# A fused attention and mixture kernel on one core: the inner weight w_in is loaded, multiplied and used by quarters of its columns

## The chip, the cores and the metric

The kernel runs on one core of one Trainium2 chip, as one program. The metric is the device time of that program in microseconds (us), the median of three runs. TensorE is called PE in the profile, its weight loads PEld, VectorE DVE, ScalarE ACT, GpSimd POOL; SP is the engine whose queue issues the loads and stores.

## The reference

Three stages follow each other; every size is fixed.

```python
# attention: q, k, v of 4 batches, 8 heads, 1152 positions, 64 wide
q_pool = q.reshape(B, H, S // 2, 2, D).mean(axis=3)
attn = softmax(q_pool @ k.T / sqrt(D)); x = (attn @ v)        # -> x: 2304 tokens x 512
# soft mixture: phi 512 x 32, w1 8 x 512 x 1024, w2 8 x 1024 x 512
logits = x @ phi
slot_input = softmax(logits, axis=0).T @ x                    # 32 slots x 512
slot_out = relu(slot_input[e] @ w1[e]) @ w2[e]                # 4 slots for each of 8 e
x = softmax(logits, axis=1) @ slot_out                        # 2304 x 512
# feed-forward: w_in 512 x 2048, w_out 2048 x 512
h = x @ w_in
g = where(h >= 1, h, where(h <= -1, 0, (h + 1) ** 2 / 4))
return g @ w_out                                              # 2304 x 512
```

## The kernel before, in words

The attention (up to about 505 us of the span) and the softmax statistics are not touched by the change. What follows them is one pass with this order.

**Weights.** `w_load` issues the loads of w1, w2 and w_in on SP's queue in the order of `wlist`, 1 MB each, into 2048-column slots that come free one after the other (`w_used`). w_in and w_out come in as float64; during the attention they are turned into float32 and stored to two scratch tensors in device memory, `wi_dr` and `wo_dr` (`cv_step`), from which they are loaded again at the end.

**Slots.** `h1` multiplies the slot inputs with w1, `ht_mm` transposes the result on PE, `s2o(e, x)` multiplies with w2. `soT` is the transposed slot output, 128 x 4 x 32.

**M.** Since x = c @ slot_out has rank 32, x @ w_in is computed as c @ M with M = slot_out @ w_in, a 32 x 2048 matrix. The products of L916 make it as 4 groups of 32 rows by 512 columns, from all of `soT` and all four chunks of w_in; ACT copies it rounded (`Mhi`), DVE takes the rest (`Mlo`), and `Mrep(j)` spreads one group of 512 columns over the 128 partitions by a product with a selection matrix `Sel`, and copies it to `Mst`. `cT` is the transposed c, made by `c_xpose(n)` for thirds of the tokens.

**Feed-forward.** The tokens run in 9 blocks n of 256 (`TB`), the 2048 hidden columns in quarters qd of four chunks f of 128. `h_unit(n, qd)` makes h for a quarter (4 products on PE, two ReLU on ACT, two clamps on DVE), `g_unit` squares on ACT and adds on DVE, `g_split` rounds g on ACT (`ghi`) and subtracts on POOL (`glo`). The first eight chunks of block 0 go in six smaller pieces, `first_unit(i)`. Its call i does the front part of piece i and the end (add, round, subtract) of piece i - 1, so that call 6 only ends piece 5. `w_split(f0, f1)` rounds rows of w_out on ACT into `whi` and subtracts on DVE or POOL into `wlo`, in place. An output tile of 128 tokens is the sum over 16 chunks of three products, ghi with whi, ghi with wlo and glo with whi: `o_first(0, pos, f)` for the first four chunks of block 0, `o_part(n, tt, qd)` for all else, 12 products each.

**What sets the order.** Each engine works through its instructions in the order in which this code issues them and waits in order. `ahead(k)` runs the units of the list `units` up to number k in front of the output products; `FIRST`, `AHEAD` and `RUN` are its numbers. `warm_o` issues products that nobody reads.

## Time and profile before

| what | us |
|---|---|
| median of 3 runs (786.8 to 788.6) | 787.86 |
| the profiled execution, its own time | 788.76 |
| its span in the profile | 787.0 |
| PE busy in the span | 758.0 |
| DVE busy | 565.5 |
| ACT busy | 451.6 |
| POOL busy | 146.1 |

Busy times are sums over the whole span; the stretch that the change touches, some 45 us between 546 and 592 us, has to be read by itself.

### The profile page before, as it was taken

To read this page: it belongs to the slowest core of one execution; us is meant where nothing else is said; L and a number is where in the kernel's file an instruction comes from. 1 tells how busy PE (TensorE), PEld (TensorE's weight loads), DVE (VectorE), ACT (ScalarE), POOL (GpSimd) and SP (SyncE) were. 2 spreads that over 40 slices of the span, in tenths; PEclk is the share of its full clock that TensorE was granted. 3 is DMA by queue.
4 is the path that set the end of the run, shared out by engine and by line. 5 is a ranking of instruction groups with operands and counts; after the bars stand their busy time and mean duration, and the time that the engine had idled before them with its cause. 6 is when DMAs were issued, how large, how long until landed. Compare 5 with 4: busy or idle time off the path is not lost.

```text
span 787.0 us, 19058 instructions
## 1 busy us (share of the span) xinstructions
PE 758.0 (96%) x7896; PEld 557.9 (71%) x7896; DVE 565.5 (72%) x869; ACT 451.6 (57%) x855; POOL 146.1 (19%) x114
## 2 busy tenths in 40 slices
PE   7799999999999999999999999999789999999998
PEld 6677776766776766766766776633578888888887
DVE  6989889778889788889788883151697777666620
ACT  4347566666667566667575566401587777555620
POOL 7000000000000000000000000002574444443330
PEclk9999999999999999999999999999989999999999
DMA  8976767867789877899878826799600000000000
GB/s 215 203 185 167 190 185 189 225 187 204 196 217 246 214 179 164 232 184 241 230 175 202 220 89 235 271 333 395 241 0 27 28 28 17 11 27 27 27 28 27
DMA packets 138263, 127.11 MB, mean 162 GB/s; under 512 B 80576, under 2 KB 100288, under 8 KB 137408
## 3 DMA queue, kind: packets, MB, share of 16 engines
q1 hardware_dynamic: 138176, 125.89, 59.2%
q8 instruction: 62, 1.02, 0.5%
q14 instruction: 25, 0.20, 0.1%
HBM read 87.10 MB, written 13.11 MB: 127 GB/s over the span
## 4 chain that ended last, share of the span: by engine, by line
PE 84%; ACT 5%; DMA 4%; DVE 4%; issue 2%; SPq 1%; ACTq 0%; DVEq 0%
PE st L368 17%; PE acc L397 16%; PE mx L302 9%; PE po L1024 8%; PE po L1023 8%; PE po L1025 8%; PE acc L390 5%; ACT e L373 3%; DMA wi<-wi_dr 2%; PE h L960 2%; PE h L767 2%; PE tx L434 2%; ACT xnr L450 1%; PE tb L461 1%; DVE mp L314 1%
## 5 line engine op out<-in xcount | busy, mean ns | idle before, releaser
L373 ACT ACTIVATE e<-st 128x576 f32<-128x576 f32 x288 | 187.6, 652 | 147.6 <-PE st L368 142.9
L314 DVE TENSOR_REDUCE mp<-mx 128x1 f32<-128x576 f32 x282 | 211.0, 750 | 53.6 <-PE mx L302 50.4
L397 PE MATMUL acc<-e,vf 128*64 128x288 f32 x1152 | 198.0, 410 | 0.3 <-ACT e L373 0.3
L302 PE MATMUL mx<-K,q 128*64 128x288 f16 x1152 | 126.5, 294 | 11.5 <-ACT e L373 4.5
L368 PE MATMUL st<-q,K 128*64 128x288 f16 x1152 | 123.7, 287 | 4.1 <-DVE mp L314 2.5
L368 PE MATMUL st<-q,S 128*64 128x288 f16 x1152 | 123.7, 286 | 0.0
L302 PEld LDWEIGHTS <-q 128*64 128x64 f16 x1152 | 67.6, 110 | 69.4 <-issue 27.3
L1023 PE MATMUL po<-whi,ghi 128*128 128x512 f32 (+1 forms) x280 | 108.6, 388 | 0.0
L1024 PE MATMUL po<-wlo,ghi 128*128 128x512 f32 (+1 forms) x280 | 108.5, 388 | 0.0
L1025 PE MATMUL po<-whi,glo 128*128 128x512 f32 (+1 forms) x280 | 108.1, 386 | 0.0
L973 DVE TENSOR_TENSOR r<-cl,r 128x1024 f32<-128x1024 f32 x34 | 80.9, 2380 | 36.8 <-ACT cl L972 36.8
L979 POOL TENSOR_TENSOR glo<-r,ghi 128x1024 fp32r<-128x1024 f32 x34 | 82.1, 2414 | 95.4 <-ACT ghi L978 95.4
L270 POOL TENSOR_TENSOR qf<-qf 128x576 f32<-128x576 f32 x14 | 20.1, 1437 | 382.5 <-DMA qf<-in_q_dram 260.4
L397 PEld LDWEIGHTS acc<-e,vf 128*64 128x64 f32 x1152 | 80.3, 137 | 8.5 <-ACT e L373 2.4
L368 PEld LDWEIGHTS <-K 128*64 128x64 f16 x1152 | 70.2, 109 | 21.9 <-issue 12.7
L368 PEld LDWEIGHTS <-S 128*64 128x64 f16 x1152 | 71.4, 110 | 2.7
L380 DVE TENSOR_TENSOR es<-es,e 128x576 f32<-128x576 f32 x96 | 71.4, 745 | 2.6 <-ACT e L373 2.5
L963 ACT ACTIVATE r<-h,cols 128x512 f32<-128x512 f32 x68 | 42.9, 684 | 31.9 <-PE h L960 31.7
L1025 PEld LDWEIGHTS po<-whi,glo 128*128 128x128 f32 x280 | 53.2, 190 | 10.7
L1023 PEld LDWEIGHTS po<-whi,ghi 128*128 128x128 f32 x280 | 53.5, 191 | 9.9
L1024 PEld LDWEIGHTS po<-wlo,ghi 128*128 128x128 f32 x280 | 53.3, 190 | 9.5
L964 DVE TENSOR_SCALAR cl<-h 128x512 f32<-128x512 f32 x68 | 43.8, 685 | 15.6 <-ACT r L963 14.1
(192 smaller groups left out, 845.2 us busy)
## 6 DMA issues: line engine op xcount, KB each, us to landing
w<-in_moe_w_dram SPq DMA_DIRECT2D x31, 1024.0 KB, 7.6
vf<-in_v_dram SPq DMA_DIRECT2D x16, 576.0 KB, 5.0
kf<-in_k_dram SPq DMA_DIRECT2D x30, 288.0 KB, 3.8
f<-in_moe_w_out_dram SPq DMA_DIRECT2D x16, 512.0 KB, 5.2
f<-in_moe_w_in_dram SPq DMA_DIRECT2D x16, 512.0 KB, 5.8
qf<-in_q_dram SPq DMA_DIRECT2D x30, 256.0 KB, 4.6
S<-K SPq DMA_DIRECT2D x16, 288.0 KB, 6.2
out_dram<-ob SPq DMA_DIRECT2D x17, 256.0 KB, 2.0
```

The costliest lines, as they stand in the source:

```text
L302: nc.tensor.matmul(ps[p0:p1, i, 0:HQ], lhsT=q1[P][:, t, p0:p1], rhs=kk[:, j * HQ:(j + 1) * HQ], start=True, stop=True)
L314: nc.vector.tensor_reduce(out=mp[P][:, t, a:a + 1], in_=ps[:, :, 0:HQ], op=ALU.max, axis=AX.XY)
L368: nc.tensor.matmul(ps[c0:c0 + 64, i, 0:HQ], lhsT=kk[:, ci, c0:c0 + 64], rhs=f[:, sl[i]], start=first, stop=not first)
L373: nc.scalar.activation(out=e, in_=ps[:, :, 0:HQ], func=AF.Exp, scale=ESC)
L380: nc.vector.tensor_tensor(out=Es[P, n, h], in0=a, in1=b, op=ALU.add)
L397: nc.tensor.matmul(acc[P, i][h * 64:(h + 1) * 64, 0:HQ], lhsT=vt[P][:, h, c, :], rhs=E[P, c, h][:, i, :], start=(c == 0), stop=(c == NK - ...
L964: nc.vector.tensor_scalar(out=cl[:, a:b], in0=src, scalar1=-1.0, scalar2=1.0, op0=ALU.max, op1=ALU.min)
L973: nc.vector.tensor_tensor(out=r[:, sl], in0=cl[:, sl], in1=r[:, sl], op=ALU.add)
L979: nc.gpsimd.tensor_tensor(out=glo[n, qd][:, sl], in0=r[:, sl], in1=ghi[n, qd][:, sl].bitcast(F32), op=ALU.subtract)
L1023: nc.tensor.matmul(po, lhsT=ghi[n, qd][:, j, sl], rhs=whi[:, f, cs], start=(f == 0), stop=False)
L1024: nc.tensor.matmul(po, lhsT=ghi[n, qd][:, j, sl], rhs=wlo[:, f, cs], start=False, stop=False)
L1025: nc.tensor.matmul(po, lhsT=glo[n, qd][:, j, sl], rhs=whi[:, f, cs], start=False, stop=(f == 15))
```

## The change

w_in is stored in `wi_dr` by quarters of its 2048 columns, and each of its four loads now brings one quarter of the columns of all 512 rows. They go in turn with quarters of w_out: w_in 0, w_out 0, w_in 1, w_out 1, and so on; w_in 1 and 2 land for a while in rows of `whi` that are written only later, w_in 3 in a tile of its own. M is made by quarters: `M_piece(q)` makes 512 of its columns (as 4 groups of 128), copies and subtracts, and `Mrep(q)` spreads them, 8 products of 128 columns, with one copy by DVE. So the hidden columns of a quarter qd need M's quarter qd alone. Pieces 0 and 1 come before the output products, 2 and 3 between them; `quarter(q)` runs the units (0, 2) and (0, 3) with the w_out rows that belong to them. w2 is loaded with four consecutive rows to a partition (8 KB in one run), for which the transposes of `ht_mm` read columns 4 apart. Half of the copies of `c_xpose` go from ACT to DVE; one row of `warm_o` falls away.

```diff
--- before.py
+++ after.py
@@ -101,9 +101,9 @@
     LASTW = ("w1", 1, 0)
     wlist = [(kind, e, x) for kind in ("w1", "w2") for x in range(2) for e in range(E_) if (kind, e, x) != LASTW]
     wlist.insert(NSL, LASTW)
-    wlist += [("wi", dc, 0) for dc in range(4)]
+    wlist += [("wi", 0, 0)]
     wo_dr = dr_p.tile([128, 16, DM], F32, name="wo_dr")
-    wi_dr = dr_p.tile([4, 128, DFF], F32, name="wi_dr")
+    wi_dr = dr_p.tile([128, 4, 4, 512], F32, name="wi_dr")
     wt = {}
     nloaded, gone = 0, set()
 
@@ -121,17 +121,11 @@
             src = w1[e, :, x * 512:(x + 1) * 512].rearrange("(c p) f -> p c f", p=128)
             vw = t.rearrange("p (c f) -> p c f", c=4)
         elif kind == "w2":
-            src = w2[e, x * 512:(x + 1) * 512, :].rearrange("(c p) d -> p c d", p=128)
+            src = w2[e, x * 512:(x + 1) * 512, :].rearrange("(p c) d -> p c d", p=128)
             vw = t.rearrange("p (c d) -> p c d", c=4)
         else:
-            src, vw = wi_dr[e], t
-        if i < len(wlist) - 1:
-            nc.sync.dma_start(out=vw, in_=src)
-        else:
-
-            for hf in range(2):
-                a, b = [y.rearrange("p (j n) -> p j n", j=4)[:, :, hf * 256:hf * 256 + 256] for y in (vw, src)]
-                nc.sync.dma_start(out=a, in_=b)
+            src, vw = wi_dr[:, e], t.rearrange("p (c n) -> p c n", c=4)
+        nc.sync.dma_start(out=vw, in_=src)
         wt[kind, e, x] = vw
 
     def w_used(*keys):
@@ -205,7 +199,7 @@
                 nc.sync.dma_start(out=wo_dr[:, n, :], in_=dst)
             else:
                 dc, qr = divmod(n - 16, 4)
-                nc.sync.dma_start(out=wi_dr[dc][:, qr * 512:(qr + 1) * 512], in_=dst)
+                nc.sync.dma_start(out=wi_dr[:, qr, dc, :], in_=dst)
             if n + 3 < 32:
                 cv_load(n + 3)
 
@@ -773,8 +767,9 @@
         def ht_mm(i):
             htp[i] = sc_tile("ht0")[:, 0, :] if i == 0 else hp_tile("ht1")
             for kc in range(4):
-                nc.tensor.transpose(out=htp[i][:, kc * 128:(kc + 1) * 128], in_=h1s[i][:, kc * 128:(kc + 1) * 128],
-                                    identity=ident)
+
+                nc.tensor.transpose(out=htp[i][:, kc * 128:(kc + 1) * 128],
+                                    in_=h1s[i].rearrange("p (n k) -> p k n", k=4)[:, kc, :], identity=ident)
 
         def ht_sum(i):
             nc.vector.tensor_reduce(out=HT[:, 4 * i:4 * i + 4], in_=htp[i].rearrange("p (k d s) -> p k s d", k=4, d=4),
@@ -806,7 +801,10 @@
                     nc.tensor.transpose(out=ps[:, t * TT:(t + 1) * TT],
                                         in_=CN[:, n * 8 + 4 * i + t].rearrange("p r s -> p (r s)"), identity=ident[0:TT, 0:TT])
                 c0 = n * 768 + i * 384
-                nc.scalar.activation(out=cT[:, c0:c0 + 384], in_=ps[:, 0:384], func=AF.Copy)
+                if i:
+                    nc.vector.tensor_copy(cT[:, c0:c0 + 384], ps[:, 0:384])
+                else:
+                    nc.scalar.activation(out=cT[:, c0:c0 + 384], in_=ps[:, 0:384], func=AF.Copy)
 
         def s2o(e, x):
 
@@ -885,11 +883,21 @@
                 for r in range(4):
                     src = ident[:, 32 * j:32 * j + 32] if r // 2 == hl else zcol.to_broadcast([128, 32])
                     nc.gpsimd.tensor_copy(Sel[:, hl, j, 32 * r:32 * r + 32], src)
+
+        def wi_load(q_, t):
+            nc.sync.dma_start(out=t, in_=wi_dr[:, q_].rearrange("p c n -> p (c n)"))
+            wt["wi", q_, 0] = t.rearrange("p (c n) -> p c n", c=4)
+
+        def wo_load(q_):
+            nc.sync.dma_start(out=wlo[:, 4 * q_:4 * q_ + 4, :].bitcast(F32), in_=wo_dr[:, 4 * q_:4 * q_ + 4, :])
+
+        for q_ in range(3):
+            if q_:
+
+                wi_load(q_, whi[:, 4 * q_ + 4:4 * q_ + 8, :].bitcast(F32).rearrange("p f d -> p (f d)"))
+            wo_load(q_)
         for e in range(E_):
             s2o(e, 1)
-        pieces = [(0, 2), (2, 4), (4, 8), (8, 12), (12, 16)]
-        for f0, f1 in pieces:
-            nc.sync.dma_start(out=wlo[:, f0:f1, :].bitcast(F32), in_=wo_dr[:, f0:f1, :])
 
 
         def w_split(f0, f1):
@@ -905,25 +913,29 @@
         nc.vector.tensor_copy(soT, over_slots(hp_tile("soT"), S2sb))
         acc_x.close()
         po_p = ctx.enter_context(tc.tile_pool(name="po", bufs=4, space=PS))
-        Mp = [po_tile(f"M{i}")[:, 0:DM // 2] for i in range(2)]
+        for n in (1, 2):
+            c_xpose(n)
         wps = po_tile("warm_o")
-        for dc in range(4):
-            if dc < 2:
-                c_xpose(1 + dc)
-            for i in range(2):
-                for j in range(4):
-                    c0 = j * 512 + i * 256
-                    nc.tensor.matmul(Mp[i][32 * j:32 * j + 32], lhsT=soT[:, dc, :],
-                                     rhs=wt["wi", dc, 0][:, c0:c0 + 256], start=(dc == 0), stop=(dc == 3))
         Mst = x_p.tile([128, NTT * DM], F32R, tag="xn", name="Mst")
         Mhi, Mlo = Mst[:, DFF:DFF + DM], Mst[:, DFF + DM:DFF + 2 * DM]
-        HF = [slice(0, DM // 2), slice(DM // 2, DM)]
-        for i, sl in enumerate(HF):
-            nc.scalar.activation(out=Mhi[:, sl], in_=Mp[i], func=AF.Copy)
-            nc.vector.tensor_tensor(out=Mlo[:, sl], in0=Mp[i], in1=Mhi[:, sl].bitcast(F32), op=ALU.subtract)
-
+
+
+        def M_piece(q_):
+            ps = hp_tile(f"M{q_}")[:, 0:128]
+            for dc in range(4):
+                for j in range(4):
+                    nc.tensor.matmul(ps[32 * j:32 * j + 32], lhsT=soT[:, dc, :],
+                                     rhs=wt["wi", q_, 0][:, dc, j * 128:(j + 1) * 128], start=(dc == 0), stop=(dc == 3))
+            sl = slice(q_ * 128, (q_ + 1) * 128)
+            nc.scalar.activation(out=Mhi[:, sl], in_=ps, func=AF.Copy)
+            nc.vector.tensor_tensor(out=Mlo[:, sl], in0=ps, in1=Mhi[:, sl].bitcast(F32), op=ALU.subtract)
+
+        M_piece(0)
         w_split(0, 2)
         wx.close()
+        wi3_p = ctx.enter_context(tc.tile_pool(name="wi3", bufs=1))
+        wi_load(3, wi3_p.tile([128, 2048], F32, name="wi3"))
+        wo_load(3)
 
 
         g_p = ctx.enter_context(tc.tile_pool(name="g", bufs=6))
@@ -933,16 +945,13 @@
         NBK = NT // TB
         ghi, glo, hq = {}, {}, {}
 
-        def Mrep(j, parts):
-            for i, sl in enumerate(parts):
-                ps = hp_tile(f"Mr{j}_{i}")[:, 0:sl.stop - sl.start]
+        def Mrep(q_):
+            ps = hp_tile(f"Mr{q_}")
+            for j in range(4):
                 for hl, src in enumerate((Mhi, Mlo)):
-                    nc.tensor.matmul(ps, lhsT=Sel[:, hl, j, :], rhs=src[:, sl], start=(hl == 0), stop=(hl == 1))
-                dst = Mst[:, j * 512 + sl.start:j * 512 + sl.stop]
-                if (i + j) % 2 == 0:
-                    nc.vector.tensor_copy(dst, ps)
-                else:
-                    nc.scalar.activation(out=dst, in_=ps, func=AF.Copy)
+                    nc.tensor.matmul(ps[:, j * 128:(j + 1) * 128], lhsT=Sel[:, hl, j, :], rhs=src[:, q_ * 128:(q_ + 1) * 128],
+                                     start=(hl == 0), stop=(hl == 1))
+            nc.vector.tensor_copy(Mst[:, q_ * 512:(q_ + 1) * 512], ps)
 
 
         def h_unit(n, qd, j0, j1):
@@ -978,7 +987,7 @@
             nc.scalar.activation(out=ghi[n, qd][:, sl], in_=r[:, sl], func=AF.Copy)
             nc.gpsimd.tensor_tensor(out=glo[n, qd][:, sl], in0=r[:, sl], in1=ghi[n, qd][:, sl].bitcast(F32), op=ALU.subtract)
 
-        units = [(n, qd, 0, 4) for n in range(NBK) for qd in range(4)][2:]
+        units = [(n, qd, 0, 4) for n in range(NBK) for qd in range(4)][4:]
 
         def unit_step(i):
             if i < len(units):
@@ -1043,15 +1052,25 @@
 
         pos = o_tiles(0)
         warm_o(WARM[3])
-        Mrep(0, HF)
+        Mrep(0)
         for f in range(5):
             if f == 4:
-                warm_o(WARM[4])
+                M_piece(1)
+                break
             first_unit(f)
             if f == 1:
-                Mrep(1, [slice(0, DM)])
                 w_split(2, 4)
         nu = 0
+
+
+        def quarter(q_):
+            u, f = (0, q_, 0, 4), 4 * q_
+            Mrep(q_)
+            h_unit(*u)
+            w_split(f, f + 2)
+            g_unit(*u)
+            w_split(f + 2, f + 4)
+            g_split(*u)
 
         def ahead(n):
             nonlocal nu
@@ -1067,18 +1086,23 @@
                     if n == 0 and qd == 0:
                         for f in range(4):
                             o_first(0, pos, f)
-                            if f < 2:
-                                first_unit(5 + f)
-                                Mrep(2 + f, [slice(0, DM)])
+                            if f == 0:
+                                Mrep(1)
+                            if f < 3:
+                                first_unit(4 + f)
                             if f == 1:
                                 w_split(4, 8)
-                            ahead(FIRST[f])
+                            if f == 2:
+                                M_piece(2)
+                        quarter(2)
                         continue
-                    if n == 0 and qd < 3:
-                        w_split(4 * qd + 4, 4 * qd + 8)
-                    ahead(4 * n + qd + AHEAD + min(n, RUN))
+                    if n or qd > 1:
+                        ahead(4 * n + qd - 2 + AHEAD + min(n, RUN))
                     for tt in range(2):
                         o_part(n, tt, qd, pos[tt])
+                        if n == 0 and qd == 1 and tt == 0:
+                            M_piece(3)
+                            quarter(3)
                         if qd == 3:
                             o_out(n, tt, pos[tt])
             else:
```

Three places show how the order on the engines moves. On ACT, the first is where the first units of block 0 end (ghi_1 is the rounding of the hidden chunks 4 to 7, whi the rounding of rows of w_out, h_2 the third quarter). Before:

```order
L1008 ACTIVATE cl_1_8591<-cl_1_8591,cols 128x512
L1014 ACTIVATE ghi_1_8592<-r_1_8590 128x512 x2
L945 ACTIVATE Mst<-Mr_0_8631 128x512
L897 ACTIVATE whi<-wlo 128x512 x4
L963 ACTIVATE r_2_8649<-h_2_0_8651,cols 128x512
```

And with the change:

```order
L1017 ACTIVATE cl_1_8600<-cl_1_8600,cols 128x512
L1023 ACTIVATE ghi_1_8601<-r_1_8599 128x512
L905 ACTIVATE whi<-wlo 128x512 x4
L1023 ACTIVATE ghi_1_8601<-r_1_8599 128x512
L930 ACTIVATE Mst<-M_8644 128x128
L972 ACTIVATE r_2_8679<-h_2_0_8681,cols 128x512
```

The four roundings of w_out now stand ahead of the second ghi_1, and the copy of M's third quarter (M_8644) behind both. On DVE, the same place before (wlo is the subtraction for a row of w_out):

```order
L1013 TENSOR_TENSOR r_1_8590<-cl_1_8591,r_1_8590 128x512
L1017 TENSOR_SCALAR r_1_8590<-h_6_8609 128x512
L943 CAST Mst<-Mr_0_8618 128x512
L1013 TENSOR_TENSOR r_1_8590<-cl_1_8591,r_1_8590 128x512
L899 TENSOR_TENSOR wlo<-wlo,whi 128x512 x2
```

And with the change:

```order
L1022 TENSOR_TENSOR r_1_8599<-cl_1_8600,r_1_8599 128x512
L1026 TENSOR_SCALAR r_1_8599<-h_6_8618 128x512
L907 TENSOR_TENSOR wlo<-wlo,whi 128x512 x2
L1022 TENSOR_TENSOR r_1_8599<-cl_1_8600,r_1_8599 128x512
L931 TENSOR_TENSOR Mst<-M_8644,Mst 128x128
L954 CAST Mst<-Mr_8669 128x512
```

The last add of the first units stands behind two subtractions for w_out, and M's third quarter behind that add. On PE, the place where the output products of the second quarter of block 0 begin, before (h_3 and h_0 are the units (0, 3) and (1, 0), po the output tiles):

```order
L1032 MATMUL po_1_8534<-whi,glo_0_8548 128x512
L960 MATMUL h_3_0_8677<-cT,Mst 128x256 x2
L960 MATMUL h_3_1_8682<-cT,Mst 128x256 x2
L960 MATMUL h_0_0_8693<-cT,Mst 128x256 x2
L960 MATMUL h_0_1_8698<-cT,Mst 128x256 x2
L1023 MATMUL po_0_8533<-whi,ghi_1_8592 128x512
```

With the change, twelve products later, in the middle of that quarter:

```order
L1034 MATMUL po_0_8513<-whi,glo_1_8602 128x512
L927 MATMUL M_8717<-wi_8501,soT 32x128 x16
L952 MATMUL Mr_8736<-Mst,Sel 128x128 x8
L969 MATMUL h_3_0_8748<-cT,Mst 128x256 x2
L969 MATMUL h_3_1_8753<-cT,Mst 128x256 x2
L1032 MATMUL po_1_8514<-whi,ghi_1_8601 128x512
```

M's last quarter and its spreading, and with them the unit (0, 3), stand between the products of the two output tiles; units (0, 3) and (1, 0) no longer precede them.

## Rows read from the trace of the kernel before

**Rows 1.** The chain that ended last: start, us, what

```profile
537.41 17.11 DMA wi<-wi_dr
```

**Rows 2.** Queue of SP, and DMA issues: count, size, us to landing

```profile
530.72 5.94 SPq L129 DMA_DIRECT2D wi<-wi_dr  x3
540.07 10.59 SPq L892 DMA_DIRECT2D wlo<-wo_dr  x5
...
wi<-wi_dr SPq DMA_DIRECT2D x1, 1024.0 KB, 15.7
```

**Rows 3.** Windows: stretch, us, busy us of each engine, granted clock, DMA share, GB/s

```profile
533.00:537.40 4.40, 4.40 (x44) 1.37 (x40) 1.25 (x9) 0.00 (x0) 0.00 (x0) 1.00 1.05 384
...
554.50:560.00 5.50, 4.31 (x30) 2.94 (x30) 3.96 (x9) 3.23 (x8) 2.51 (x2) 1.00 1.03 427
...
570.00:575.00 5.00, 2.03 (x9) 1.71 (x9) 4.59 (x6) 5.00 (x11) 4.66 (x4) 0.78 0.00 0
575.00:580.00 5.00, 5.00 (x14) 3.85 (x13) 4.89 (x6) 4.69 (x7) 2.65 (x3) 0.53 0.00 0
```

**Rows 4.** Timeline of PE, 546 to 576 us

```profile
548.15 0.86 PE L806 MATMUL ct<-ident,CN 96*128 96x96 f32 x8
...
550.75 1.93 PE L916 MATMUL M<-wi,soT 128*32 128x256 f32 x32
...
556.60 0.50 PE L1006 MATMUL h<-cT,Mst 128*128 128x256 f32 x2
...
573.45 1.39 PE L960 MATMUL h<-cT,Mst 128*128 128x256 f32 x4 [2.97 <-DVE cl L964]
574.65 0.63 PE L1023 MATMUL po<-whi,ghi 128*128 128x512 f32 x1
```

**Rows 5.** Timeline of PE, two shorter stretches

```profile
582.49 0.64 PE L960 MATMUL h<-cT,Mst 128*128 128x256 f32 x4
582.96 0.40 PE L1023 MATMUL po<-whi,ghi 128*128 128x512 f32 x1
...
588.90 0.40 PE L1023 MATMUL po<-whi,ghi 128*128 128x512 f32 x1
```

**Rows 6.** Timeline of DVE

```profile
548.35 0.29 DVE L905 COPY soT<-soT 128x128 f32<-128x128 f32 x1 [1.17 <-DMA wi<-wi_dr]
...
558.02 1.54 DVE L1013 TENSOR_TENSOR r<-cl,r 128x256 f32<-128x256 f32 x1
...
560.15 0.41 DVE L1013 TENSOR_TENSOR r<-cl,r 128x256 f32<-128x256 f32 x1
...
565.88 0.68 DVE L1017 TENSOR_SCALAR r<-h 128x512 f32<-128x512 f32 x1
566.48 0.67 DVE L943 CAST Mst<-Mr 128x512 fp32r<-128x512 f32 x1
...
573.92 2.37 DVE L899 TENSOR_TENSOR wlo<-wlo,whi 128x512 fp32r<-128x512 f32 x2
...
580.79 2.49 DVE L973 TENSOR_TENSOR r<-cl,r 128x1024 f32<-128x1024 f32 x1 [0.77 <-ACT cl L972]
```

**Rows 7.** Timeline of ACT

```profile
555.27 0.38 ACT L922 ACTIVATE Mst<-M 128x256 fp32r<-128x256 f32 x1 [1.09 <-PE M L916]
...
569.59 2.18 ACT L897 ACTIVATE whi<-wlo 128x512 fp32r<-128x512 f32 x4
571.67 1.25 ACT L963 ACTIVATE r<-h,cols 128x512 f32<-128x512 f32 x2
...
576.03 1.16 ACT L972 ACTIVATE cl<-cl,cols 128x1024 f32<-128x1024 f32 x1
...
578.65 1.06 ACT L978 ACTIVATE ghi<-r 128x1024 fp32r<-128x1024 f32 x1 [0.31 <-DVE r L973]
```

**Rows 8.** Timeline of POOL

```profile
556.76 2.51 POOL L899 TENSOR_TENSOR wlo<-wlo,whi 128x512 fp32r<-128x512 f32 x2 [12.20 <-ACT whi L897]
...
570.81 6.62 POOL L899 TENSOR_TENSOR wlo<-wlo,whi 128x512 fp32r<-128x512 f32 x4 [0.23 <-ACT whi L897]
```

## The prediction, made before the changed kernel was run

> **What bounds the kernel now.** I read the chain of work that ended last first. It has one long step that is no engine's: from 537.41 a load of w_in, 17.11 us [rows 1]. SP's queue says why: a 1 MB piece of w_in issued at 530.72 lands 15.7 us later [rows 2], so by that time the transfers stand in a row, and the last of the four pieces is the last of the row. Until it has landed M isn't complete, and the first h starts only at 556.60 [rows 4]. This is the wait that the change attacks.
>
> The windows say what follows. PE has no gap while it works on w2 (4.40 of 4.40 us) [rows 3]; it is full again from 575 on, but there at a granted clock of 0.53 (1.2 GHz in place of 2.4 for most of it), and it stood still for 2.97 us ahead of that [rows 3, 4]. In between it waits for ACT, DVE and POOL, which share out the first units and the splitting of w_out: from 570 to 575 ACT is busy for 5.00 of 5.00 us and DVE for 4.59 [rows 3]. So two things bound the stretch: first the load, then three engines that work in order. From 583 on PE runs through (24 products and a unit fill the 5.94 us to 588.90 [rows 5]) and sets the end; what the change is worth is how much sooner or later PE reaches a place from which its remaining work is the same in both kernels. I take the first product of the fourth quarter (qd 3) of block 0, at 588.90 [rows 5]; what PE has done by then is the same list of units and products. All times below are on the clock of this trace.
>
> **The start of M.** `soT` is there at 548.35 + 0.29 = 548.6 [rows 6]. Both remaining pairs of `c_xpose` now stand ahead of M, the first ends at 548.15 + 0.86 = 549.0 [rows 4], the second some 0.9 later, 549.9. M's quarter is a quarter of the old work, of which half took 1.93 [rows 4]: 1.0, so 550.9. ACT's copy of 256 columns took 0.38 [rows 7]; for 128 I take 0.3 (between half of it and the whole), the same for DVE's subtraction: 551.5. `Mrep` is 8 products of 128 columns. No such product is in the trace. Below it can cost half of one of 256 columns, above as much as one of 512. Four of 256 columns take 582.96 - 582.49 = 0.47, 0.117 each; 24 of 512 stand between 582.96 and 588.43 (588.90 less the 0.47 of a unit), 0.228 each [rows 5]. I take 0.117, since each has its own weights as those of 256 have: 0.94 for eight, of which the last waits for the subtraction: 552.4. DVE's copy takes 0.67 [rows 6], and the first h starts at 553.2 instead of 556.60: **3.4 us earlier**.
>
> The Trainium skill has a price for these products: "TensorE: Matmul & The Clock Gate", section Back-to-back issue gap, gives about 81 ns for a pair of weight load and product of 128 columns. By that eight cost 0.65, and the three spreadings that lie on the path would be 0.9 us cheaper in all, 791.0 in place of the forecast below; no run so far shows such a product.
>
> The data are there. w_in 0 lands at 530.72 + 15.7 = 546.4 [rows 2], before `soT`; the pieces behind it follow at 427 GB/s [rows 3], 2.5 us each: w_out 0 at 549, w_in 1 at 551.5, w_out 1 at 554, w_in 2 at 556.5, w_out 2 at 559, w_in 3 at 561.5, w_out 3 at 564. Each is needed later than that (w_in 1 at about 554, the others below). On SP's queue the last three of w_in now stand behind the wait of the first w_out piece; that piece was issued at 540.07 already [rows 2], with some 6 us of transfers still ahead of it, so nothing runs dry. The longer rows of w2 land sooner (384 GB/s for rows of 2 KB against 427 for 8 KB [rows 3]), but PE is full there [rows 3] and soT waits for PE: worth nothing. The transposes of `ht_mm` now load weights whose columns stand 4 apart; nothing in the trace does that. Nothing if the stride is free, 2.8 us if each of the eight loads takes four times 0.117; I take nothing, since as many values are loaded. c_xpose's copies on DVE lie in time in which it waited for M.
>
> **The first units, with M's second quarter among them.** Before, from the first h to the end of the last front part (565.88 + 0.68 = 566.56 [rows 6]) it took 9.96. The same pieces remain, with a break: piece 4 needs M's quarter 1, which PE makes after piece 3. Copy, subtraction, spreading, DVE's copy and the h product follow each other: 0.3 + 0.3 + 0.94 + 0.67 + 0.4 = 2.6, in which DVE has no other unit's work. About 1 us comes back: the add of 558.02 took 1.54 instead of 0.41 [rows 6] because POOL's subtractions ran until 556.76 + 2.51 = 559.27 [rows 8], and these now run some 3 us before the adds. Net +1.6: 553.2 + 9.96 + 1.6 = 564.8, **1.8 earlier** than 566.56.
>
> **The third quarter of M behind the w_out rows.** `w_split(4, 8)` now comes ahead of the end of the last piece, and M's quarter 2 behind that end. ACT rounds the four rows in 2.18 [rows 7]. DVE's two subtractions can start at 565.4, after the first of them, and cost 2.37 as a pair beside POOL [rows 6]: 567.8. POOL needs 6.62 for four [rows 8], 3.3 for its two, from about 566.0: 569.3. The add of the last piece has two inputs in SBUF and waits for POOL, as the one of 558.02 did, which ended 0.29 after POOL's pair: so it ends at about 569.9. Then round 0.6, copy of M 0.3, subtraction 0.3, the rest of the spreading 0.9, DVE's copy 0.67, h 0.47: the first product of quarter 1 at 573.4, against 574.65 [rows 4]: **1.2 earlier**. PE has ended `o_first` by about 566 (564.8 less half a microsecond for the last products' inputs, plus 1.4 for the six) and waits for M's subtraction until 571, some 5 us; before, its wait there was 2.97.
>
> **The fourth quarter of M in the middle of quarter 1.** Before, from 574.65 to 588.90 there were 48 products and two units: 48 x 0.228 + 2 x 0.47 = 11.9, and 2.3 more for the low clock. With the change there are 48 products, four units, M 3 and its spreading: 10.9 + 1.9 + 1.0 + 0.9 = 14.7 at full clock, and a wait. PE ends M 3 at 573.4 + 12 x 0.228 + 1.0 = 577.1. ACT comes to its copy only after `quarter(2)`: from 573.1 two ReLU 1.25, two roundings 1.1, square 1.16 (576.6), two roundings 1.1 (577.7) [rows 7], then the rounding of g, 1.06, which needs DVE's add of 1024 elements: behind the square, and 2.49 when POOL is at work, as at 580.79 [rows 6]; I take 1.6, so the add ends at 578.2, the rounding at 579.3, the copy of M 3 at 579.6. DVE does another subtraction for w_out behind its add, 1.2 to 1.8: 580.0, and M's at 580.3. The spreading ends at 581.2, the copy at 581.9, the unit (0, 3) at 582.4. Between 577.1 and 582.4 PE has only 1.4 us of work: 3.9 lost. Then 12 products 2.7, two units 0.9, 24 products 5.5, a unit 0.5: 592.0 against 588.90, **3.1 later**.
>
> **The clock.** It fell to half (0.78, then 0.53 [rows 3]) when PE had stood for 2.97 us after a stretch of interrupted work. The wait of 5 us at 566 is longer, so I expect half clock from about 571 for as long as before. That makes 12 products cost 5.2 instead of 2.7, but PE then only comes to M's fourth quarter when ACT and DVE are ready for it. Between nothing and 2.7 (the next 12 products too): I take 0.9. Sum: 3.1 + 0.9 = **4.0 us slower**. The execution profiled took 788.76, 0.9 more than the median of the runs, so the forecast for the median is 787.86 + 4.0 = **791.9**.
>
> **The rivals.** *Faster, 786.1, chance 0.12.* The early start carries through. It needs one thing: the spreading of M's quarter 2 follows o_first at once, because ACT and DVE come to its copy before 566. Then quarter 1 starts at 566.1 + 0.94 + 0.67 + 0.47 = 568.2, the clock stays up, and with the same wait for M 3 (9.3 from the first h of quarter 2) the place in question is reached at 587.1, 1.8 sooner. It turns where the gap of PE after o_first is about 3 us shorter than I make it. For it speaks the rule in the Trainium skill, "Trainium Kernel Development and Optimization", section Best Practices, to overlap loads with compute; the wait of rows 1 is just that. Against it speaks the order on DVE and ACT, where four rows of w_out now stand ahead.
>
> *The same within 0.2% (1.6 us; less can't be told from no change here), 789.0, chance 0.12.* The clock stays up and DVE's and POOL's blocking in quarter(2) costs 2 us less than I count: 3.1 - 2.0 = 1.1. An add that meets no POOL, as the one of 560.15 [rows 6], would do it.
>
> *Slower still, 794.6, chance 0.12.* The products of 128 columns cost 0.228: 0.9 more for each of the three spreadings on the path, 2.7; the strided transposes at their upper bound give the same.
>
> *The change does not bring the start forward*, for instance since w_in 0 lands late: then the 3.4 are missing too and it is 795; I put it into the last case.
>
> **How the numbers follow.** The forecast, 2 to 6 us slower, has 0.64: 791.9, its own range 789.9 to 793.9 (clock 0 to 2.7, break of the first units 0.6 to 2.6). Slower by over 0.2% in all 0.64 + 0.12 = 0.76, same 0.12, faster 0.12. The range for 8 in 10 leaves out the faster case and the upper half of the slowest, 0.12 + 0.06: 787.0 to 795.0.
>
> **What would show it.** First h at about 553, nearly 3.5 us earlier; no wait of PE for a load of w_in after the first; a gap of PE of 4 to 5 us ahead of the third spreading, ended by DVE's subtraction, which stands behind two subtractions for w_out; a second gap after M 3; clock 0.5 in a window after the first gap; the first product of quarter 3 at about 592 to 593. The prediction is wrong if PE goes from o_first into quarter 2 without that gap, or if the h products of quarter 3 are ready when PE comes to them.

## The result, and the profile after

The changed kernel took 797.24 us (median of 4 runs, 796.3 to 799.55) against 788.04 for the kernel before: ratio 1.0114, 95% interval 1.009 to 1.0139, **slower by 9.2 us**. Six more runs of it in the control below gave 796.21 (792.27 to 796.6; ratio 1.0085, 1.0057 to 1.0113). The forecast was 791.9, and 795.0 the end of its range: the direction was right, the size less than half of it. The execution profiled is the longest of its four, 799.55 with a span of 797.8.

First the timeline of PE of the changed kernel (start us, us, engine, line, tiles, shape, count, idle time ahead and what ended it):

```profile
555.42 0.73 PE L1015 MATMUL h<-cT,Mst 128*128 128x256 f32 x4 [0.78 <-DVE Mst L954]
...
556.70 1.08 PE L927 MATMUL M<-whi,soT 128*32 128x128 f32 x32 [0.55 <-PE h L1015]
...
561.07 1.97 PE L952 MATMUL Mr<-Mst,Sel 128*128 128x128 f32 x8 [1.40 <-ACT Mst L930]
...
575.75 2.08 PE L952 MATMUL Mr<-Mst,Sel 128*128 128x128 f32 x8 [3.73 <-ACT Mst L930]
578.61 1.22 PE L969 MATMUL h<-cT,Mst 128*128 128x256 f32 x4 [0.78 <-DVE Mst L954]
579.63 0.63 PE L1032 MATMUL po<-whi,ghi 128*128 128x512 f32 x1
...
583.59 1.08 PE L927 MATMUL M<-wi,soT 128*32 128x128 f32 x32
...
585.61 0.33 PE L952 MATMUL Mr<-Mst,Sel 128*128 128x128 f32 x1 [0.94 <-ACT Mst L930]
586.25 1.00 PE L952 MATMUL Mr<-Mst,Sel 128*128 128x128 f32 x7 [0.31 <-DVE Mst L931]
...
599.85 0.40 PE L1032 MATMUL po<-whi,ghi 128*128 128x512 f32 x1
```

The start of M came as forecast: no wait of 17 us for a load is left, and the first h stands 4.89 us behind the start of the copy of soT (550.53), where it stood 8.25 behind it before [rows 4, 6]. Each spreading after the first is waited for: M's second quarter is multiplied by 557.8, and its spreading starts at 561.07; the third waits 3.73 us. The releaser named is ACT's copy of M (L930) each time, and the queues of ACT and DVE show why it is late. The timeline of ACT, with the columns as above:

```profile
560.43 0.42 ACT L1023 ACTIVATE ghi<-r 128x256 fp32r<-128x256 f32 x1 [0.50 <-DVE r L1022]
560.75 0.26 ACT L930 ACTIVATE Mst<-M 128x128 fp32r<-128x128 f32 x1
...
569.51 2.18 ACT L905 ACTIVATE whi<-wlo 128x512 fp32r<-128x512 f32 x4
574.90 0.63 ACT L1023 ACTIVATE ghi<-r 128x512 fp32r<-128x512 f32 x1 [3.21 <-DVE r L1022]
575.44 0.26 ACT L930 ACTIVATE Mst<-M 128x128 fp32r<-128x128 f32 x1
```

The timeline of DVE over the same place:

```profile
570.16 3.04 DVE L907 TENSOR_TENSOR wlo<-wlo,whi 128x512 fp32r<-128x512 f32 x2 [0.63 <-ACT whi L905]
573.12 1.75 DVE L1022 TENSOR_TENSOR r<-cl,r 128x512 f32<-128x512 f32 x1
575.73 0.29 DVE L931 TENSOR_TENSOR Mst<-M,Mst 128x128 fp32r<-128x128 f32 x1 [0.86 <-ACT Mst L930]
```

And that of POOL:

```profile
570.92 3.40 POOL L907 TENSOR_TENSOR wlo<-wlo,whi 128x512 fp32r<-128x512 f32 x2
```

The copy of 0.26 us at 575.44 stands behind the rounding at 574.90, this behind DVE's add (1.75 us at 573.12, while POOL subtracts up to 574.32), and that behind two subtractions for w_out (3.04 us at 570.16). This is the chain that the prediction drew for the third quarter. What it did not draw is in the windows of 5 us (busy us of PE, PEld, DVE, ACT and POOL with their instructions, granted clock, DMA share, GB/s), in the third column from the end, the clock:

```profile
516.00:521.00 5.00, 4.55 (x27) 1.52 (x30) 3.13 (x6) 0.84 (x1) 0.00 (x0) 0.66 0.84 247
...
560.00:565.00 5.00, 3.15 (x12) 2.73 (x13) 2.07 (x5) 0.58 (x2) 2.90 (x4) 0.66 0.36 147
565.00:570.00 5.00, 5.00 (x38) 3.86 (x40) 3.16 (x6) 2.67 (x5) 1.05 (x2) 0.66 0.00 0
570.00:575.00 5.00, 2.02 (x22) 1.20 (x14) 4.71 (x3) 1.78 (x5) 4.32 (x3) 1.00 0.00 0
575.00:580.00 5.00, 3.47 (x13) 3.21 (x14) 0.98 (x2) 1.25 (x3) 1.27 (x1) 0.52 0.00 0
...
590.00:595.00 5.00, 5.00 (x22) 4.12 (x21) 4.24 (x4) 4.51 (x8) 3.34 (x3) 0.77 0.00 0
```

It lies at 1.00 in whole windows and at 0.5 (1.2 GHz) in between; narrower windows put the low stretches at 561.6 to 568.4, 575.2 to 582.0 and 588.9 to 592.3. The first begins half a microsecond after PE's wait of 1.40 us, the second inside the wait of 3.73, the third after waits of 0.94, 0.31 and 0.78 (586 to 588). Before there was one such stretch [rows 3]. The fall at 516 to 521 (517.2 to 520.6) lies ahead of the units that the change moves; of 13 executions profiled here, two show it (this one and e8 below), and the control, the same program, does not, so it is chance of an execution: at most 1.7 us, half of its 3.4, of the 10.8 by which this span is longer than before's.

The stretch that decides, from the start of soT's copy on DVE over the first h and the first product of quarter 1 (q1) to the first of quarter 3 (q3), each from the timelines (before: [rows 4 to 6]):

| kernel | soT to h | h to q1 | q1 to q3 | soT to q3 | time, us | ratio to before, 95% |
|---|---|---|---|---|---|---|
| before | 8.25 | 18.05 | 14.25 | 40.55 | 787.7 to 788.5 | |
| forecast (soT to q3 without the clock's 0.9) | 4.85 | 20.2 | 18.6 | 43.65 | 791.9 | |
| after | 4.89 | 24.21 | 20.22 | 49.32 | 797.24 | 1.009 to 1.0139 |
| e9, control (after again) | 4.89 | 23.27 | 20.19 | 48.35 | 796.21 | 1.0057 to 1.0113 |
| e4, warming products | 4.89 | 20.89 | 18.72 | 44.51 | 792.49 | 1.0048 to 1.0076 |
| e1, 8 KB rows alone | 6.69 | 17.43 | 13.20 | 37.32 | 785.48 | 0.9965 to 0.9986 |
| e2, third quarter moved | 4.88 | 16.39 | 21.43 | 42.70 | 790.86 | 1.0021 to 1.0048 |
| e3, all quarters moved | 5.46 | 17.43 | 20.55 | 43.44 | 790.82 | 1.0022 to 1.005 |
| e5, loads out of turn | 4.89 | 22.93 | 18.79 | 46.61 | 795.16 | 1.0075 to 1.0103 |
| e6, order mended | 5.47 | 17.31 | 14.54 | 37.32 | 786.21 | 0.995 to 0.999 |
| e7, 2 KB rows | 4.89 | 22.98 | 20.18 | 48.05 | 794.63 | 1.0065 to 1.0098 |
| e8, fourth quarter moved | 4.89 | 27.50 | 14.82 | 47.21 | 794.89 | 1.0069 to 1.01 |
| e10, second quarter moved | 5.46 | 20.31 | 18.74 | 44.51 | 793.33 | 1.0045 to 1.0095 |
| e11, mended, 2 KB rows | 6.25 | 17.42 | 14.45 | 38.12 | 786.59 | 0.9968 to 0.9996 |

From q3 to the end of the span it is 197.9 us in after, 198.1 in before and 197.9 to 198.2 in the runs between them; in e1, e6 and e11 it is 198.7 to 199.0, so these three give back 0.6 to 0.9 of what they gain up to q3.

### The profile page after: what moved, and what is told of

Same layout as the page of the kernel before. It is cut to its first block, busy times and chain, and to the rows that moved or that the text cites. A ratio compares the mean times of both kernels' runs of the same rounds, so it can differ in the third digit from the quotient of the medians.

```text
span 797.8 us, 19206 instructions
## 1 busy us (share of the span) xinstructions
PE 766.8 (96%) x7974; PEld 566.5 (71%) x7974; DVE 566.1 (71%) x876; ACT 450.0 (56%) x851; POOL 144.3 (18%) x114
## 4 chain that ended last, share of the span: by engine, by line
PE 85%; ACT 5%; DVE 4%; DMA 3%; issue 2%; SPq 1%; ACTq 0%; DVEq 0%
PE st L362 17%; PE acc L391 16%; PE mx L296 8%; PE po L1033 8%; PE po L1032 8%; PE po L1034 8%; PE acc L384 5%; ACT e L367 3%; PE h L969 2%; PE h L761 2%; PE s2o L817 2%; PE tx L428 2%; ACT xnr L444 1%; DMA q<-qn 1%; PE tb L455 1%
## 5 line engine op out<-in xcount | busy, mean ns | idle before, releaser
L391 PE MATMUL acc<-e,vf 128*64 128x288 f32 x1152 | 197.9, 410 | 0.4 <-ACT e L367 0.3
L982 DVE TENSOR_TENSOR r<-cl,r 128x1024 f32<-128x1024 f32 x34 | 79.2, 2331 | 38.5 <-ACT cl L981 38.5
L1034 PEld LDWEIGHTS po<-whi,glo 128*128 128x128 f32 x280 | 53.3, 190 | 10.8
```

Source lines behind the costliest of these rows:

```text
L391: nc.tensor.matmul(acc[P, i][h * 64:(h + 1) * 64, 0:HQ], lhsT=vt[P][:, h, c, :], rhs=E[P, c, h][:, i, :], start=(c == 0), stop=(c == NK - ...
L982: nc.vector.tensor_tensor(out=r[:, sl], in0=cl[:, sl], in1=r[:, sl], op=ALU.add)
L1034: nc.tensor.matmul(po, lhsT=glo[n, qd][:, j, sl], rhs=whi[:, f, cs], start=False, stop=(f == 15))
```

## The experiments

The theory after the result: the copies of M wait behind other work in the queues of ACT and DVE, which are worked through in order (called order below), and the clock falls around the waits that this makes (called clock). The rivals: the loads in turn, w2's rows, the transposes and the many small products. The edits are shown shortened; `...` and comments stand for code left out.

**e1, the rows alone.** The kernel before with two edits of the change:

```diff
-src = w2[e, x * 512:(x + 1) * 512, :].rearrange("(c p) d -> p c d", p=128)
+src = w2[e, x * 512:(x + 1) * 512, :].rearrange("(p c) d -> p c d", p=128)
-    in_=h1s[i][:, kc * 128:(kc + 1) * 128], identity=ident)
+    in_=h1s[i].rearrange("p (n k) -> p k n", k=4)[:, kc, :], identity=ident)
```

> The kernel before with two parts of the change alone: w2 read in 8 KB rows, and the strided columns of h1 that the ht transposes then take. In the profile of after, the stretch up to the end of the s2o products is 2.2 us longer than before (548.5 against 546.25), with the granted clock at 0.5 from 517.2 to 520.6. Theory A, the clock's fall there is chance of that execution and the two edits cost 0.2 us (two groups of transposes of 0.68 for 0.59): 788.2 us, between 787.4 and 789.0. Rival B, the edits themselves cost the 2.2 us: 790.2 us, and the clock falls during the h1 products of this profile too.

Neither: it is *faster* than before, 785.48, and the clock stays up at 517. The timeline of SP's queue shows where from (issues start, us, count). The kernel before, eight pieces of w2, and, from a narrower stretch, the last of them by itself:

```profile
517.75 12.87 SPq L129 DMA_DIRECT2D w<-in_moe_w_dram  x8
...
528.09 2.54 SPq L129 DMA_DIRECT2D w<-in_moe_w_dram  x1
```

e1, the same eight, the last of them, and three of w_in:

```profile
517.10 7.19 SPq L129 DMA_DIRECT2D w<-in_moe_w_dram  x8
...
523.97 0.33 SPq L129 DMA_DIRECT2D w<-in_moe_w_dram  x1
524.83 3.37 SPq L129 DMA_DIRECT2D wi<-wi_dr  x3
```

In rows of 2 KB each of the last three issues takes 2.4 to 2.6 us, in rows of 8 KB 0.33 (there the eight are spread over 7.19 us because each waits for PE to free its slot), so w_in's first load is issued at 524.83 instead of 530.72 [rows 2]. For a kernel that waits for w_in's last piece [rows 1] that is worth 1.56 us up to the first h (6.69 for 8.25). Of the 1.67 more up to q3, 1.05 lie behind q1, and there the clock tells: it is low for 2.4 us behind q1 in e1 (up to 574.4) and for 5.0 in before (up to 579.7). Half of the difference, 1.3 us, accounts for the 1.05. In e1 (windows; before in [rows 3]):

```profile
570.00:575.00 5.00, 4.19 (x13) 3.36 (x14) 5.00 (x8) 5.00 (x9) 4.68 (x3) 0.66 0.00 0
```

Over all executions the mean granted clock is 0.991 in e1 and 0.990 in before. So part of the 2.4 us is clock; why it falls for a shorter time is not shown.

**e2, the third quarter moved** ahead of the split of w_out's parts 4 to 7:

```diff
-if f == 1: w_split(4, 8)
-if f == 2: first_unit(6); M_piece(2)
-quarter(2)                      # Mrep(2); h_unit; ...
+if f == 1: first_unit(6); M_piece(2)
+quarter(2)                      # Mrep(2); w_split(4, 8); h_unit; ...
```

> After, with one place of the order changed: M's third quarter and the last step of the first units are issued ahead of the split of w_out's parts 4 to 7, which then stands behind the spreading of that quarter. Theory A, M's copies wait behind other work in the in-order queues of ACT and DVE: the 3.73 us that TensorE waits ahead of the third spreading shrink to under 1, o_first's end at 572 to quarter 1's first product falls from 7.6 to about 4, and the time falls by 3 to 5 us to between 792 and 794. Rival B, the split is needed by quarter 1 and its place doesn't matter: the wait reappears ahead of quarter 1's first product, and the time stays within 1 us of 797. Rival C, the half clock is the loss: the third spreading still runs at 0.25 us a product and less than 2 us come back.

Theory A, and more than it: 790.86. The spreading follows o_first at once, q1 comes 6.9 us sooner than in the control, and the clock stays up until 579.7. The wait turns up again in part ahead of the fourth spreading (timeline of PE):

```profile
567.02 1.30 PE L952 MATMUL Mr<-Mst,Sel 128*128 128x128 f32 x8
...
576.95 0.33 PE L952 MATMUL Mr<-Mst,Sel 128*128 128x128 f32 x1 [2.46 <-ACT Mst L930]
```

**e3, all quarters moved up.** As e2, and:

```diff
 M_piece(0)
+M_piece(1)
 ...
 Mrep(2)
+M_piece(3)
 w_split(4, 8)
```

> As the run before it, and M's second quarter is multiplied right behind the first, ahead of the first units, and M's fourth right behind the third's spreading, ahead of quarter 2's units; only the spreadings stay where after has them. Theory A, order in the queues: the waits ahead of the second spreading (1.40 us) and the fourth (0.94 us, and 0.31 inside it) go too, at the price of some 1 us more ahead of the first h; the time falls to between 787 and 791, so that all but 0 to 3 us of the loss is given back. Rival B, the loads in turn set the pace: M's second quarter waits for a transfer (it landed at 551.6) and the time stays at 792 or above. Rival C, the clock: three stretches at the half clock stay after 560, and the time stays at 792 or above though the waits are gone.

790.82: the upper end of theory A, and no better than e2. PE no longer waits for a copy of M, but for the cast behind the fourth spreading, which DVE reaches only after an add (1.61 us) and a subtraction for w_out (1.75) (timeline of PE):

```profile
574.63 1.00 PE L953 MATMUL Mr<-Mst,Sel 128*128 128x128 f32 x8
...
579.20 0.74 PE L970 MATMUL h<-cT,Mst 128*128 128x256 f32 x4 [3.57 <-DVE Mst L955]
```

The chain goes PE (M), ACT (copy), DVE (subtraction), PE (spreading), DVE (cast), PE (h); it has to stand ahead of the other work in both queues, at both of its ends.

**e4, warming products in the waits.** After with products that nobody reads:

```diff
+warm_o(6)                       # 18 ahead of Mrep(2), 4 ahead of Mrep(3)
 Mrep(1)
+warm_o(3)                       # behind the other two as well
```

> After, in its own order, with products of the warming kind (128 columns, 0.18 us each at the full clock) in the places where TensorE waits: 6 ahead of the second spreading, 18 ahead of the third, 4 ahead of the fourth, 3 behind each. Their results are not used. They fill the waits and cannot shorten them. Theory A, order: the chains on ACT and DVE keep their length, and only what ran at the half clock gets shorter, by the rows 0.6 of the second spreading, 0.7 of the third, 0.5 of its h products, 1.2 and 1.7 of quarter 1's, of which part lies beside the chains: 794 to 796. Rival C, the clock is the loss: the granted clock stays at 1.0 from 556 to 600 and 5 to 6 us come back, 791 to 792. Rival D, the filling itself lengthens the path: over 798.

In the execution profiled the granted clock stays at 1.00 in every window from 550 to 600, of which three:

```profile
560.00:565.00 5.00, 4.94 (x51) 3.82 (x51) 3.81 (x7) 2.91 (x6) 1.19 (x2) 1.00 0.00 0
570.00:575.00 5.00, 4.58 (x29) 3.75 (x28) 1.99 (x4) 2.30 (x6) 1.27 (x1) 1.00 0.01 3
575.00:580.00 5.00, 3.65 (x47) 2.64 (x45) 4.22 (x5) 3.87 (x7) 3.61 (x3) 1.00 0.00 0
```

The timeline of PE, with the first h, the spreadings, q1 and q3:

```profile
552.40 0.74 PE L1015 MATMUL h<-cT,Mst 128*128 128x256 f32 x4 [0.78 <-DVE Mst L954]
...
558.04 1.32 PE L952 MATMUL Mr<-Mst,Sel 128*128 128x128 f32 x8
...
570.62 1.32 PE L952 MATMUL Mr<-Mst,Sel 128*128 128x128 f32 x8 [0.35 <-ACT Mst L930]
...
573.30 0.40 PE L1032 MATMUL po<-whi,ghi 128*128 128x512 f32 x1
...
579.42 0.33 PE L952 MATMUL Mr<-Mst,Sel 128*128 128x128 f32 x1 [1.09 <-ACT Mst L930]
...
592.02 0.40 PE L1032 MATMUL po<-whi,ghi 128*128 128x512 f32 x1
```

The filling lengthens nothing (the second spreading starts 10.53 us behind soT's copy, 10.52 in the control). From soT to q3 it takes 44.51 us, 3.84 less than the control and 4.8 less than after; the median is 3.72 less than the control's (792.49, between what A and C expected). The interval of the ratio meets the control's, not that of the first four runs; against all ten executions of after, with a mean of 796.1, the mean of e4's six is 792.8. So clock and order are both in it: about 3.8 us of clock; the other 7.3 us (h to q3 39.61 against 32.30 before, which has a fall of its own) stay with the clock at full, and the mended order below takes 7.8 of those 39.61 away.

**e5, the loads out of turn; e7, w2's old rows; e8, the fourth quarter moved alone.**

```diff
 # e5
-wi 0, wo 0, wi 1, wo 1, wi 2, wo 2
+wi 0, wi 1, wi 2, wo 0, wo 1, wo 2
 # e7: the edit of e1 undone in after
 # e8
-Mrep(2); h_unit(0, 2); ...    M_piece(3); Mrep(3); h_unit(0, 3)
+Mrep(2); M_piece(3); Mrep(3); h_unit(0, 2); ...    h_unit(0, 3)
```

> After, with the loads of w_in's first three quarters issued ahead of those of w_out's first three, so no longer in turn. Each of the seven transfers takes 2.5 us, so w_out's first quarter lands some 5 us later (at about 554 instead of 549.1 in after's own time) and w_in's third 5 us earlier. Theory A, no load of after is waited for and the in-turn order is worth nothing: 797, between 796 and 798.5, the last one if the first split of w_out (it starts at 553.2) has to wait the 1 us. Rival B, the order of the loads is what breaks M up: at most 795. Rival C, w_out's first quarter gets onto the path with all 5 us: over 800.

> After, with w2 read in 2 KB rows again and the ht transposes of before. With 8 KB rows alone the kernel before got 2.4 us faster, because its w_in landed 3.25 us earlier (551.3 instead of 554.5) and the first h waits for it. Theory A, in after no load is waited for (w_in's first quarter landed at 546.6 and is used at 551.8), so the rows are worth nothing there: 797, between 796 and 798. Rival B, the rows are worth 2 us wherever they stand: 799 to 800.

> After, with M's fourth quarter and its spreading issued right behind the third's spreading, ahead of quarter 2's units, and nothing else moved. The fourth step alone: from the first product of quarter 1 to that of quarter 3 after takes 20.2 us and before 14.25. Theory A, the fourth quarter's own chain makes the 6 us: the stretch falls to 15 to 16, 1.5 to 2.5 us are paid ahead of it, 793 to 795. Rival B, the copies only find their queues full at another place (in the run with all pieces moved the fourth spreading's copy was waited for 3.6 us on DVE): 796 to 798. Rival C, the clock falls in the longer wait ahead of quarter 1 and eats the gain: a stretch at the half clock over the products of quarter 1, 795 to 797.

All three came out 1 to 1.6 us under the control below (e9, 796.21), with intervals inside its own: no effect that can be told. The ranges for "worth nothing" in e5 and e7 were set around the 797.2 of the first four runs, and both came out under them. After waits for no load at either row length, and out of turn for one, 0.34 us of ACT's. So the loads cost after nothing that these runs can tell. In e8 the fourth step shrinks as theory A has it (20.2 to 14.8), and the time lies in A's range; but what is moved ahead of q1 runs at the half clock and costs 4.2 there (27.50 for 23.27), not the 1.5 to 2.5 expected, which is what rival C drew (timeline of PE):

```profile
575.08 2.08 PE L952 MATMUL Mr<-Mst,Sel 128*128 128x128 f32 x8 [3.74 <-ACT Mst L930]
577.10 1.94 PE L927 MATMUL M<-wi,soT 128*32 128x128 f32 x32
579.43 2.08 PE L952 MATMUL Mr<-Mst,Sel 128*128 128x128 f32 x8 [0.40 <-ACT Mst L930]
```

**e9, the control.** After itself, unchanged.

> The changed kernel itself once more, beside the others. Three runs, with the loads out of turn (795.2), with w2's old rows (794.6) and with the fourth quarter moved up (794.9), each came out 2 to 2.6 us under the 797.2 of the first measurement. Theory A, none of the three edits is worth anything by itself and 797.2 was high because two or more of its four executions had the clock fall at 517 too: 794.5 to 796. Theory B, each of the three gives back 2 us: 796.5 to 798.

796.21, between the ranges of A and B and nearer to A's; whether falls at 517 made the first four runs long is not shown, as only one of them has a trace. The profiled one of these has no fall at 517 but four stretches of low clock later (windows):

```profile
555.00:560.00 5.00, 4.87 (x39) 3.45 (x30) 3.33 (x8) 3.15 (x9) 4.50 (x5) 0.73 0.82 341
560.00:565.00 5.00, 4.22 (x14) 3.48 (x14) 2.96 (x6) 1.03 (x2) 1.27 (x2) 0.66 0.01 5
...
570.00:575.00 5.00, 2.08 (x8) 1.85 (x8) 2.29 (x3) 0.79 (x2) 2.29 (x2) 0.64 0.00 0
...
585.00:590.00 5.00, 5.00 (x20) 4.12 (x20) 3.19 (x4) 4.38 (x7) 1.60 (x2) 0.66 0.01 3
```

The first of them begins at 554.3, after waits of PE of only 0.78 and 0.54 us. The same program took 792.27 to 799.55 in ten executions, and the shortest had the highest mean clock (0.987), the longest the lowest (0.978). The scatter of this kernel goes with the clock; in this execution it was low in four stretches, in the one profiled first in three and at 517.

**e10, the second quarter moved alone:** of e3's edit the first line only.

> After, with M's second quarter multiplied right behind the first and nothing else moved: the break of the first units alone. Theory A, the 1.40 us that TensorE waits ahead of the second spreading and the fall of the clock behind it are the loss of the second step: the wait goes, 1 us is paid ahead of the first h, and 2 to 3 us come back against the control. Rival B, the first units are paced by the elementwise work on ACT and DVE (in the run with all pieces moved o_first's first products waited 1.67 us for ghi instead): within 1 us of the control, the wait only changes its name.

793.33, 2.9 under the control, as theory A has it, though the intervals overlap; soT to q3 is 3.84 shorter. The second spreading is no longer waited for, 0.6 is paid ahead of the first h, and the third, reached sooner, is waited for longer (timeline of PE):

```profile
557.27 1.00 PE L953 MATMUL Mr<-Mst,Sel 128*128 128x128 f32 x8
...
569.62 2.08 PE L953 MATMUL Mr<-Mst,Sel 128*128 128x128 f32 x8 [4.38 <-ACT Mst L930]
```

**e6, the order mended.** After's loads and quarters of M, but the units in before's order, so that every copy of M stands where ACT and DVE come to it early:

```diff
 M_piece(0)
+M_piece(1)
 ...                             # first pieces: Mrep(1) behind piece 1, as before
-M_piece(1); break
+M_piece(2); first_unit(4)       # in place of the warming products
 ...                             # o_first: Mrep(2), Mrep(3) behind pieces 5 and 6, as before
+M_piece(3)                      # behind piece 5
-quarter(2), quarter(3)
+units 2, 3 by ahead(), w_split(4, 8) and on, all as before
```

> After's loads and quarters of M, with the units in the order of the kernel before: M's second quarter right behind the first, the third among the first units where before has warming products, the fourth ahead of the third spreading; the spreadings, the eight first pieces, the splits of w_out and the later units stand where before has them. Theory A, the loss is the order of the copies and the clock that falls in the waits it makes, and both go: the start comes 2 to 3 us earlier than in before, three spreadings cost 0.5 us each more than before's, 785 to 787, at or below the kernel with 8 KB rows alone (785.5). Rival B, M by quarters costs in itself (32 products of 128 columns, eight copies for two): 788 to 790. Rival C, the clock falls here too: one stretch at the half clock ahead of quarter 1 as in before; two or more and over 788.

Theory A: 786.21, faster than before. No window of 5 us from 550 to 600 has a clock under 1.00. The timeline of PE, with the first h, q3 and the three longest waits that are left:

```profile
552.76 0.50 PE L1016 MATMUL h<-cT,Mst 128*128 128x256 f32 x2 [0.78 <-DVE Mst L955]
...
562.50 1.32 PE L953 MATMUL Mr<-Mst,Sel 128*128 128x128 f32 x8 [0.85 <-ACT Mst L930]
...
569.13 1.10 PE L970 MATMUL h<-cT,Mst 128*128 128x256 f32 x4 [1.54 <-DVE cl L974]
...
579.02 0.50 PE L1035 MATMUL po<-whi,glo 128*128 128x512 f32 x1 [1.71 <-POOL glo L989]
...
584.61 0.40 PE L1033 MATMUL po<-whi,ghi 128*128 128x512 f32 x1
```

So M by quarters with the loads in turn costs nothing by itself that shows in the time; where its pieces were put did.

**e11, the mended order with w2's 2 KB rows.**

> The kernel with the order mended (786.2), with w2 in 2 KB rows and the ht transposes of before. Theory A, with the loads in turn w_in's first quarter is there in time at either row length, so the rows are worth nothing: 786.2, within 0.8. Rival B, the three later transfers come some 3 us later and the third and fourth quarter of M, which this kernel multiplies at 555 and 558, wait for them: 787 to 789.

786.59, theory A's time. Loads are waited for now (0.57 and 1.17 us), as rival B had it, but the time doesn't show it (timeline of PE):

```profile
549.62 1.08 PE L927 MATMUL M<-whi,soT 128*32 128x128 f32 x32 [0.57 <-DMA whi<-wi_dr]
...
559.56 1.08 PE L927 MATMUL M<-wi,soT 128*32 128x128 f32 x32 [1.17 <-DMA wi<-wi_dr]
```

Rows alone (e1), quarters with the loads in turn alone (e11) and both (e6) give 1.1 to 2.4 us against before, and both together no more than one. That fits with all three shortening the same wait for w_in, and with DVE and POOL setting the pace behind it (in e6 PE waits 1.71 us for POOL at 579.02); no run here separates the two. The simplest of the three, e1, is the version to keep: it beats the kernels before and after (ratio 0.9975 to before), and e6 (0.997) can't be told from it.

## Why the prediction came out wrong

**The start of M: right.** 4.85 us forecast, 4.89 measured. A product of 128 columns cost about what was chosen, 0.117: of the fourth spreading one alone took 0.33 and the seven behind it 1.00, so they stand (1.00 - 0.33) / 6 = 0.112 apart. By the Trainium skill's figure of about 81 ns ("TensorE: Matmul & The Clock Gate", section Back-to-back issue gap) the seven would take 0.33 + 6 x 0.081 = 0.82, an estimate; the trace disagrees. Strided transposes: in e1 the product behind four of them starts 0.68 us after the first instead of 0.59, 0.2 in all, near the lower bound taken. That w2's longer rows are worth nothing was right for this kernel (e7), but left out what they are worth without the rest of the change: 2.4 us (e1).

**The first units and the third quarter: right at full clock.** From first h to the end of the last front part: 11.56 forecast, 12.0 in e4 (552.40 to 564.41). Of the 1 us that was to come back there only 0.4 did: the next pair of POOL's subtractions still meets an add (1.14 us at 556.24 in e4, where before took 1.54 [rows 6]). On to q1: 8.6 forecast, 8.9 in e4. The wait ahead of the third spreading, 5 us forecast, is 3.73 in after and 3.98 in the control, and stands behind the two subtractions named.

**The fourth quarter: right at full clock.** q1 to q3 18.6 forecast, 18.72 in e4.

**The clock: the step that failed.** The prediction has half clock once, "for as long as before", takes 0.9 for it and 2.7 as its upper bound. It fell three times (four in the control) and cost 3.8 us by e9 against e4, 4.8 by the execution profiled first, the fall at 517 not counted. Step by step, from the timelines of PE:

| from | to | after | control | e4 | after less e4 |
|---|---|---|---|---|---|
| first h | third spreading | 20.33 | 19.39 | 18.22 | 2.1 |
| third spreading | q1 | 3.88 | 3.88 | 2.68 | 1.2 |
| q1 | fourth spreading | 5.98 | 5.98 | 6.12 | -0.1 |
| fourth spreading | q3 | 14.24 | 14.21 | 12.60 | 1.6 |

The fall that the prediction counted, in the wait ahead of the third spreading, cost 1.2, inside its 0 to 2.7. That the slow products of quarter 1 are hidden by the chains on ACT and DVE was right (third line), but half clock also stretches links of those chains themselves: the spreading (2.08 for 1.32) and the h products (1.22 for 0.73). What failed is that the falls ahead of it, in the first step, and behind the fourth spreading got nothing, although the sum itself had both places as new gaps: they cost 3.7 together, 2.8 in the control. In after they fell after waits of 1.40 and of 0.94, 0.31 and 0.78; before waits up to 1.26 us without a fall and has its one fall in the wait of 2.97. With the clock at 1.00 through the whole stretch the kernel takes 791.72 (e4's profiled execution; the median of its six, with mean clocks from 0.991 to 0.996, is 792.49), where the sum without the clock's term gives 787.9 + 3.1 = 791.0.

**The rivals.** "Faster" turned on the third spreading following o_first at once. In e2 that happens, and its q1 is at 16.4 us from h, where this rival had 15.0; the fourth quarter takes it back. "The same" needed the clock to stay up; in e4 it did, and the time is still 4.6 us over before's (792.49 for 787.89). The prices of "slower still" (794.6) and of a start that is not brought forward (795) came nearest to the result, by luck: products of 128 columns cost 0.112, not 0.228, the strided transposes 0.2, not 2.8, and the start did come forward. What stays open is which waits let the clock fall, which differs from execution to execution: of the same order of instructions, e6 waits 1.54 us ahead of quarter 1 with no fall behind it, and e11 1.52 with one (0.66 from 570 to 575); and e2 waits the same 1.40 ahead of the second spreading as after, with no fall until 579.7.

## What to carry to other kernels

A chain that crosses engines is only as early as its last place in any queue that is worked through in order: when a matrix is cut into quarters so that its loads overlap, put each quarter's copies ahead of the bulk work of ACT and DVE, at both ends of the chain, or the waiting moves on instead of going away. Count each new gap of PE as a possible fall of the clock, once per gap, with the products behind it at about twice their time (here 2.08 for 1.32 and 1.94 for 1.08). And try the cheapest way of shortening a wait by itself first: here longer rows of an earlier load gave as much as those rows and the whole rearrangement together, in the best order tried (e1, e6).

## What was not expected of the hardware

Row length was paid at the issuing queue: the last three of eight transfers of 1 MB held SP for 2.4 to 2.6 us each in rows of 2 KB, for 0.33 in rows of 8 KB, and the loads behind them were issued 5.9 us later (0.65 of it is that the whole trace of before lies later there: 517.75 for 517.10). The same program's time scattered by 0.9% (792.27 to 799.55) with its mean granted clock between 0.987 and 0.978, while the mended ones stayed within 3.3 us (e6, e11).
